# One program for attention and two mixture layers: the second layer's vector, scalar and GpSimd work issued by seven slots, and its weight sums cut in four

## The chip, the core and the metric

The kernel runs on one core of a Trainium2 chip. The core has TensorE (PE; its weight loads are listed apart as PEld), VectorE (DVE), ScalarE (ACT), GpSimd (POOL) and the queue of SyncE (SP), which issues nearly all DMAs here. The engines run on their own and meet at semaphores; each takes its instructions strictly in the order in which the program gives them. The metric is the device time of one execution in microseconds (us). The kernel before was run three times: 1477.61, 1478.47 and 1479.58 us, median 1478.47.

## What is computed

```python
attn = attention in chunks of 64 tokens       # batch 4, 8 heads, 576 tokens, head size 64
x = attn.reshape(2304, 512)
h = np.maximum(x @ w_in, 0.0)                 # first layer: 512 -> 2048
x = h * h @ w_out                             #              2048 -> 512
p = domain_probs / domain_probs.sum(-1)       # second layer: 4 experts
for e in range(4):
    h = np.maximum(x @ w1[e], 0.0)            # 512 -> 1024
    out += p[:, e:e + 1] * (h @ w2[e])        # 1024 -> 512
```

All matrices are float32. The kernel splits every operand of the large products into a rounded high part and the remainder (a low part), and adds three products (high by high, high by low, low by high), so each product stands as three matmuls.

## The kernel before

**First layer.** Attention, the first layer and the preparation of the second layer's weights are written as one row of ticks, `r` = 0 to 85. From tick 20 on a tick holds 12 matmuls of step `m` of the first product (`l1`) and 12 of step `m - 1` of the second (`l2`); 80 steps in all, over blocks of 384 or 512 tokens (8 of 20 steps have 384). Between them stands a chain: ACT takes the ReLU of PSUM into the tile `r` (L308), DVE squares it (L309), ACT rounds the high part (L313), DVE takes the low part (L314), and `l2` of the next tick reads both. The raw weights of the first layer arrive as float64 words; 20 blocks of them are turned into float32 after 170 us (L129 to L152), with three instructions of POOL for each block.

**Jobs.** The second layer's weights are four experts by four quarters of the 1024 columns, with two matrices each: 32 `job`s, one started every second tick from tick 20. Before the second layer can use Strassen's form (seven products of half matrices instead of eight), a job loads the four quarters (three DMAs), POOL forms four sums (L469), and the seven pieces are split into high and low parts and stored to DRAM. Before, a job moves on once at the end of every tick: load; one tick later the sums; one tick later the first half of the split (ACT rounds 896 columns at L475, DVE and POOL take the remainder of 448 columns each at L478, SP stores 896 KB at L481); one tick later the second half. All engines take their parts in program order, so an ACT instruction of a job stands between the ACT instructions of the chain above.

**Second layer.** 48 units `n`: three groups of 768 tokens, times four experts, times four quarters of the 1024 columns (`j` = 0 to 3). A unit has seven slots `u`. In a slot PE does six matmuls of 384 columns (`c_unit`, L525: one Strassen product of this unit's hidden values) and then nine of 256 columns (`d_unit`, L618: three products of the unit before; in slot 0 those of the unit two before). `c_finish` turns the seven sums in three PSUM banks (`b`, `c`, `d`) into seven pairs of high and low tiles: `s1` and `s3` are made by DVE in slot 5, `s2` by POOL from `s1`, and `s4` by DVE from `s2` in slot 6; `split` rounds on ACT (L558) and takes the remainder on POOL (L559). `d_finish` adds the finished banks of token block `t` into `uw` and the outputs: after product 6 the bank x = 1 into `uw` (DVE L655, in units with `j` = 0 ACT L653), after product 5 the bank x = 0 (DVE L657), then the scaled parts. When `j` = 3, `uw` is put into the outputs (L637, L683). PE may not go on in a bank's other half until the add that reads the whole bank is done. In slot 0 the products (2, 4) and (2, 2) need the adds that followed (2, 6) and (2, 5) in slot 6.

**What sets the order.** Nothing is scheduled by a program: each engine gets its instructions in the order in which this code runs. In a slot of before it is: PE's six, `c_finish` of this slot, then for each of three products its nine matmuls' share and its `d_finish`.

Of the kernel before, what the change touches and what calls it, by code (L numbers as in the profile page):

```python
# [18 lines left out]
P = 128  # L19
# [13 lines left out]
HALF = 384  # L33
# [11 lines left out]
def tile_kernel(ctx, tc, q, k, v, moe_w_in, moe_w_out, moe2_p, moe2_w1, moe2_w2, out):  # L45
# [245 lines left out]
    def l1(i):  # L291
# [4 lines left out]
        for kk in range(KD):  # L296
# [16 lines left out]
        nc.scalar.copy(hi[:, :T], r[:, :T])  # L313
        nc.vector.tensor_tensor(  # L314
            out=lo[:, :T], in0=r[:, :T], in1=hi[:, :T].bitcast(F32), op=ALU.subtract
# [100 lines left out]
    def y_split(sp, i):  # L416
        h, l = y_slot(i)
        a = comb[sp][i]
        nc.scalar.copy(h, a)
        eng = nc.vector if sp == 0 or i % 2 == 0 else nc.gpsimd  # L420
        eng.tensor_tensor(out=l, in0=a, in1=h.bitcast(F32), op=ALU.subtract)
        yield
# [17 lines left out]
    def job_load(which, n):  # L440
        e, j = divmod(n, NP)
        r = late["jb"].tile([P, 8, 2 * P], F32, tag="raw", name="jraw", bufs=2)
# [17 lines left out]
        1: ((4, 0, 3, ALU.add), (5, 4, 1, ALU.subtract), (6, 1, 0, ALU.subtract), (7, 2, 5, ALU.subtract)),  # L460
        2: ((4, 0, 1, ALU.subtract), (5, 3, 4, ALU.subtract), (6, 0, 3, ALU.subtract), (7, 2, 5, ALU.subtract)),
    }

    def job(which, n):

        r = job_load(which, n)
        yield
        for o, a, b, op in SUMS[which]:
            nc.gpsimd.tensor_tensor(out=r[:, o], in0=r[:, a], in1=r[:, b], op=op)  # L469
        yield  # L470
        c = NW // 2
        for part in range(2):
            x = r.rearrange("p s c -> p (s c)")[:, 2 * P + part * c:2 * P + (part + 1) * c]
            w = late["jb"].tile([P, 2, c], F32R, tag="split", name="jsplit", bufs=2)
            nc.scalar.copy(w[:, 0], x)  # L475
            for i, eng in enumerate((nc.gpsimd, nc.vector)):
                cs = slice(i * c // 2, (i + 1) * c // 2)
                eng.tensor_tensor(  # L478
                    out=w[:, 1, cs], in0=x[:, cs], in1=w[:, 0, cs].bitcast(F32), op=ALU.subtract
                )  # L480
            nc.sync.dma_start(out=kept[which, n][:, :, part * c:(part + 1) * c], in_=w.bitcast(F32))  # L481
            yield
# [20 lines left out]
    UNITS = ((0, Y11), (1, Y21), (4, T2), (3, T1), (5, T3), (6, Y22), (2, T4))  # L503
    A11, A12, A22, S1, S2, S3, S4 = range(7)
    B11, B21, B22, R1, R2, R3, R4 = range(7)
    g, st = {}, {}

    def c_unit(n, u):
        ws, ys = UNITS[u]
        if u == 0:  # L510
            st["b"] = bank("t")
# [4 lines left out]
        elif u == 1:  # L516
            st["c"] = bank("h")
        elif u == 3:
            st["d"] = bank("t")
        p = st["bcbdbdb"[u]][:, :HALF]  # L520
# [14 lines left out]
    def snap(nm, p):  # L535
        s = st[nm] = temp(nm)
        nc.scalar.copy(s, p)  # L537

    def keep(nm, p):
        s = st[nm] = temp(nm)  # L540
        nc.scalar.activation(out=s, in_=p, func=AF.Relu)

    def high(n, i, p):
        nc.scalar.activation(out=g[n][i][0], in_=p, func=AF.Relu)  # L544

# [6 lines left out]
    def relu_with(nm, p, other, op):  # L552
        s = st[nm] = temp(nm)
        nc.vector.scalar_tensor_tensor(out=s, in0=p, scalar=0.0, in1=st[other], op0=ALU.max, op1=op)  # L554

    def split(n, i, nm):
        h, l = g[n][i]
        nc.scalar.copy(h, st[nm])  # L558
        nc.gpsimd.tensor_tensor(out=l, in0=st[nm], in1=h.bitcast(F32), op=ALU.subtract)  # L559

    def c_finish(n, u):
        b, c, d = (st[x][:, :HALF] if x in st else None for x in "bcd")
        if u == 0:
            snap("u1", b)
        elif u == 1:
            nc.vector.tensor_tensor(out=c, in0=c, in1=st["u1"], op=ALU.add)
            high(n, A11, c)
            keep("a11", c)
            low(n, A11, c)
        elif u == 2:  # L570
            snap("u2", b)
        elif u == 3:
            snap("u3", d)
        elif u == 4:
            c = st["c"] = bank("h")
            c = c[:, :HALF]
            nc.vector.tensor_tensor(out=c, in0=b, in1=st["u3"], op=ALU.add)
            keep("a22", c)
            high(n, A22, c)
            low(n, A22, c)  # L580
        elif u == 5:
            nc.vector.tensor_tensor(out=d, in0=d, in1=st["u2"], op=ALU.add)
            relu_with("s1", d, "a22", ALU.add)
            relu_with("s3", d, "a11", ALU.subtract)
            s = st["s2"] = temp("s2")
            nc.gpsimd.tensor_tensor(out=s, in0=st["s1"], in1=st["a11"], op=ALU.subtract)  # L586
            split(n, S3, "s3")
            split(n, S2, "s2")
            split(n, S1, "s1")
        elif u == 6:  # L590
            high(n, A12, b)
            relu_with("s4", b, "s2", ALU.subtract)
            split(n, S4, "s4")

    def c_last(n):
        low(n, A12, st["b"][:, :HALF])
# [26 lines left out]
    owed = []  # L623

    def d_flush(n, t):
        sp, m = divmod(n, NU)
        e = m // NP
        r1 = rows[sp][t + 3]
        p1 = prob[:, r1 // P, e:e + 1]
# [283 lines left out]
```

## Time and profile before

| what | value |
|---|---|
| median of three runs | 1478.47 us |
| the profiled execution | 1476.51 us, of which the span is 1474.7 us |
| PE busy in the span | 1272.3 us (86%) |
| DVE, POOL, ACT busy | 897.2, 781.1, 652.4 us |
| first layer from tick 20 to its end | about 170 to 576.5 us |
| start of the second layer | 576.5 to 595.5 us |
| its units up to the last slot of products | 595.5 to 1451 us |
| mean granted TensorE clock | 0.949 |

A row of a timeline gives the start and the time of some instructions that follow one another, their engine, line, operation and tiles, and in square brackets how long the engine stood idle before them and what released it. A list of waits adds these idle times up. No engine but PE is busy for more than 61% of the span, and PE's idle time is what can be won. A PE that waits also loses time afterwards where the granted clock has fallen.

### The profile page before, as it was taken

The numbers are of one execution on the slowest core, as the hardware profiler recorded it, in microseconds if no ns is written. First come the engines' busy times: TensorE is split into PE (matmuls) and PEld (weight loads), VectorE is DVE, ScalarE is ACT, GpSimd is POOL, SyncE is SP. The second block draws the span as 40 slices with busy tenths as digits, with TensorE's granted clock in tenths as the row PEclk, the third lists the DMA queues.
The fourth block names the chain that finished last, engine by engine and source line by source line (L and its number), as shares of the span: only waits on it lengthen the run. The fifth ranks groups of instructions, "written<-read, shape, count | busy, mean of one in ns | idle before, by whom it ended". The sixth has DMA issues, their size and how long they took to land.

```text
span 1474.7 us, 22299 instructions
## 1 busy us (share of the span) xinstructions
PE 1272.3 (86%) x8344; PEld 1160.9 (79%) x8344; DVE 897.2 (61%) x1439; ACT 652.4 (44%) x1271; POOL 781.1 (53%) x771
## 2 busy tenths in 40 slices
PE   6999977987896998898988878988888889888896
PEld 5888866766675876888888878888888788888786
DVE  7866765586566556355656555656565556565655
ACT  5555543343343334444444444444444444444442
POOL 3400686676667466254655453556554535454544
PEclk8999989999999899899999999999999999999998
DMA  9752256676574666755556556556565465565642
GB/s 216 164 113 68 71 180 218 205 230 205 203 255 149 223 240 212 302 200 200 204 196 216 193 191 243 200 200 215 190 229 186 180 243 205 196 227 185 235 153 93
DMA packets 134972, 288.79 MB, mean 196 GB/s; under 512 B 64977, under 2 KB 93649, under 8 KB 128721
## 3 DMA queue, kind: packets, MB, share of 16 engines
q1 hardware_dynamic: 132240, 286.72, 57.5%
q8 instruction: 65, 1.06, 0.3%
q10 hardware_dynamic: 2624, 0.66, 0.2%
q14 instruction: 43, 0.34, 0.1%
HBM read 223.91 MB, written 63.44 MB: 195 GB/s over the span
## 4 chain that ended last, share of the span: by engine, by line
PE 40%; DVE 17%; POOL 13%; DMA 10%; issue 8%; ACT 8%; SPq 3%; POOLq 0%; DVEq 0%; ACTq 0%
PE psa L618 17%; PE pst L525 10%; DMA jraw<-in_moe_w 6%; POOL jraw L469 4%; PE psh L525 4%; DVE s L554 3%; PE psa L330 3%; POOL jsplit L478 3%; PE psh L298 3%; POOL s L586 3%; ACT ar L558 2%; ACT ar L544 2%; DMA w2d<-jsplit 2%; DVE uw L657 2%; DVE o L679 2%
## 5 line engine op out<-in xcount | busy, mean ns | idle before, releaser
L525 PE MATMUL pst<-ar 128*128 128x384 f32 x1728 | 350.2, 338 | 6.0 <-ACT u L537 3.4
L525 PEld LDWEIGHTS pst<-ar 128*128 128x128 f32 x1728 | 292.0, 190 | 6.7 <-ACT u L537 3.7
L330 PE MATMUL psa<-ar 128*128 128x512 f32 (+1 forms) x960 | 247.4, 397 | 56.0 <-ACT ar L313 32.7
L618 PE MATMUL psa<-w2x,ar 128*128 128x256 f32 x1512 | 216.2, 288 | 65.0 <-DVE uw L655 61.5
L618 PE MATMUL psa<-ar 128*128 128x256 f32 x1512 | 225.2, 293 | 54.3 <-DVE uw L655 28.7
L618 PEld LDWEIGHTS psa<-ar 128*128 128x128 f32 x1512 | 211.3, 198 | 66.7 <-DVE uw L655 32.4
L618 PEld LDWEIGHTS psa<-w2x,ar 128*128 128x128 f32 x1512 | 202.7, 195 | 76.9 <-DVE uw L655 69.1
L330 PEld LDWEIGHTS psa<-ar 128*128 128x128 f32 x960 | 180.2, 199 | 105.2 <-ACT ar L313 44.3
L667 POOL TENSOR_TENSOR o<-o,x 128x256 f32<-128x256 f32 x135 | 101.0, 748 | 240.0 <-ACT x L666 223.6
L559 POOL TENSOR_TENSOR ar<-s,ar 128x384 fp32r<-128x384 f32 x192 | 195.3, 1045 | 4.6 <-ACT ar L558 4.6
L558 ACT CAST ar<-s 128x384 fp32r<-128x384 f32 x192 | 93.7, 512 | 179.8 <-DVE s L554 170.8
L469 POOL TENSOR_TENSOR jraw<-jraw 128x256 f32<-128x256 f32 x128 | 108.8, 871 | 97.8 <-DMA jraw<-in_moe_w 95.3
L478 DVE TENSOR_TENSOR jsplit<-jraw,jsplit 128x448 fp32r<-128x448 f32 x64 | 63.9, 998 | 117.8 <-ACT jsplit L475 112.9
L657 DVE TENSOR_TENSOR uw<-psa,uw 128x512 f32<-128x512 f32 x144 | 95.1, 688 | 64.4 <-PE psa L618 47.6
L298 PE MATMUL pst<-ar 128*128 128x512 f32 (+1 forms) x576 | 132.1, 380 | 0.0
L298 PEld LDWEIGHTS pst<-ar 128*128 128x128 f32 x576 | 111.1, 197 | 14.6
L475 ACT CAST jsplit<-jraw 128x896 fp32r<-128x896 f32 x64 | 60.2, 940 | 115.0 <-POOL jraw L469 110.6
L143 POOL TENSOR_TENSOR raw<-raw 128x512 f32<-128x512 f32 x32 | 35.0, 1093 | 142.6 <-DVE raw L142 84.3
L548 DVE SCALAR_TENSOR_TENSOR ar<-psh,ar 128x384 fp32r<-128x384 f32 x96 | 53.6, 558 | 90.3 <-ACT ar L544 45.1
L537 ACT COPY u<-pst 128x384 f32<-128x384 f32 x144 | 69.1, 480 | 83.6 <-PE pst L525 81.2
L586 POOL TENSOR_TENSOR s<-s,a 128x384 f32<-128x384 f32 x48 | 48.9, 1019 | 107.4 <-DVE s L554 83.3
L314 DVE TENSOR_TENSOR ar<-r,ar 128x512 fp32r<-128x512 f32 (+1 forms) x80 | 76.2, 953 | 39.8 <-ACT ar L313 38.2
(112 smaller groups left out, 1878.1 us busy)
## 6 DMA issues: line engine op xcount, KB each, us to landing
ar<-w1d SPq DMA_DIRECT2D x48, 1792.0 KB, 7.3
ar<-w2d SPq DMA_DIRECT2D x48, 896.0 KB, 7.1
w2x<-w2d SPq DMA_DIRECT2D x48, 896.0 KB, 6.8
w1d<-jsplit SPq DMA_DIRECT2D x32, 896.0 KB, 4.9
w2d<-jsplit SPq DMA_DIRECT2D x32, 896.0 KB, 5.2
raw<-in_moe_w_in SPq DMA_DIRECT2D x16, 512.0 KB, 5.9
raw<-in_moe_w_out SPq DMA_DIRECT2D x16, 512.0 KB, 4.8
jraw<-in_moe_w SPq DMA_DIRECT2D x32, 256.0 KB, 5.2
```

The costliest lines, as they stand in the source:

```text
L298: nc.tensor.matmul(ph[:, :T], lhsT=w[:, kk, :], rhs=x[tb][:, kk, :], start=(kk == 0 and n == 0), stop=(kk == KD - 1 and n == 2),)
L314: nc.vector.tensor_tensor(out=lo[:, :T], in0=r[:, :T], in1=hi[:, :T].bitcast(F32), op=ALU.subtract)
L330: nc.tensor.matmul(o, lhsT=w, rhs=y, start=(f == 0 and n == 0), stop=(f == G - 1 and n == 2))
L469: nc.gpsimd.tensor_tensor(out=r[:, o], in0=r[:, a], in1=r[:, b], op=op)
L478: eng.tensor_tensor(out=w[:, 1, cs], in0=x[:, cs], in1=w[:, 0, cs].bitcast(F32), op=ALU.subtract)
L525: nc.tensor.matmul(p, lhsT=w[:, kk, :], rhs=y[:, kk, :], start=(kk == 0 and z == 0 and u in (0, 1, 3)), stop=(kk == 1 and z == 2 and u in ...
L558: nc.scalar.copy(h, st[nm])
L559: nc.gpsimd.tensor_tensor(out=l, in0=st[nm], in1=h.bitcast(F32), op=ALU.subtract)
L586: nc.gpsimd.tensor_tensor(out=s, in0=st["s1"], in1=st["a11"], op=ALU.subtract)
L618: nc.tensor.matmul(p, lhsT=w, rhs=y, start=(k in (1, 7) and z == 0), stop=(k in (3, 4) and z == 2), skip_group_check=True,)
L657: nc.vector.tensor_tensor(out=uw, in0=pb[n, t, 0], in1=uw, op=ALU.add)
L667: nc.gpsimd.tensor_tensor(out=o1[:, :2 * P], in0=o1[:, :2 * P], in1=x, op=ALU.add)
```

## The change

Four things change.

- **Slots.** `d_finish` is gone. Its parts have names (`B`: bank x = 1 into `uw`; `A`: bank x = 0; `x1`, `x0`: scaled copies; `o1`, `o0`, `O`: into the outputs; `W`, `F`: the end of an expert), and two tables, BEFORE and AFTER, say in which slot each is written, ahead of or behind the slot's nine matmuls. `c_finish` is cut into nine steps: slots 7 and 8 are slots 0 and 1 of the next unit. The `s4` pair and the low part of A12 move there. The splits of the next token group (`y_split`) are spread over slots 1 to 10.
- **Jobs.** A job now moves on by half ticks: the sums two ticks after the load, two quarters of the split at the end of the tick after the next, their stores half a tick later, the other two quarters half a tick after that. Each quarter is 448 columns on ACT, and its remainder is wholly POOL's or wholly DVE's. Three buffers each for the loaded and the split tiles, instead of two. One store is 448 KB; a job has four.
- **Squares.** From tick 20 on `l1` leaves the square in its PSUM bank instead of the tile `r`, and ACT and DVE read it there.
- The order of the seven weight pieces in memory is another one (UNITS, SUMS, R3 and B11 to R4). PE's instructions stand as before.

```diff
+        sq = r if "x" not in late else ph
         nc.vector.scalar_tensor_tensor(
-            out=r[:, :T], in0=ph[:, :T], scalar=0.0, in1=r[:, :T], op0=ALU.max, op1=ALU.mult
+            out=sq[:, :T], in0=ph[:, :T], scalar=0.0, in1=r[:, :T], op0=ALU.max, op1=ALU.mult
         )
...
-        yield
+        yield 4
         for o, a, b, op in SUMS[which]:
             nc.gpsimd.tensor_tensor(out=r[:, o], in0=r[:, a], in1=r[:, b], op=op)
-        yield
-        c = NW // 2
+        yield 3
+        c = NW // 4
...
-            w = late["jb"].tile([P, 2, c], F32R, tag="split", name="jsplit", bufs=2)
+            w = late["jb"].tile([P, 2, c], F32R, tag="split", name="jsplit", bufs=3)
             nc.scalar.copy(w[:, 0], x)
...
+            eng = nc.vector if part % 2 else nc.gpsimd
+            eng.tensor_tensor(out=w[:, 1], in0=x, in1=w[:, 0].bitcast(F32), op=ALU.subtract)
...
+            if part % 2:
+                yield 1
+                for o, w in done:
+                    nc.sync.dma_start(out=o, in_=w)
+                done = []
+                yield 1
...
+        elif at == 6:
             split(n, S3, "s3")
+            nc.scalar.activation(out=g[n][A12][0], in_=b, func=AF.Relu)
             split(n, S2, "s2")
+        elif at == 7:
             split(n, S1, "s1")
+            relu_with(n, "s4", b, "s2", ALU.subtract)
+            low(n, A12, b)
+        elif at == 8:
             split(n, S4, "s4")
...
+    BEFORE = {4: ((0, "o1"), (0, "W"), (1, "W")), 5: ((1, "o1"),), 7: ((2, "W"),), 8: ((2, "o1"),), 9: ((2, "o0"),)}
+    AFTER = {
+        1: ((0, "B"),), 2: ((1, "B"),), 3: ((0, "A"), (1, "A"), (0, "x1")), 4: ((0, "O"), (1, "x1")),
+        5: ((1, "O"),), 6: ((2, "B"), (2, "A")), 7: ((2, "x1"), (2, "x0"), (0, "F")), 8: ((1, "F"),),
+        10: ((2, "F"),),
+    }
+    SPLITS = {1: Y11, 2: Y21, 3: T2, 4: T1, 7: T3, 8: Y22, 10: T4}
```

On DVE in the second layer, at the end of an ordinary unit (slots 5 and 6, and the first of slot 0), there stood before, `s4` ahead of the two adds into `uw`:

```order
L554 SCALAR_TENSOR_TENSOR s1_6200<-pst_6145,a22_6176 128x384
L554 SCALAR_TENSOR_TENSOR s3_6202<-pst_6145,a11_6110 128x384
L679 SCALAR_TENSOR_TENSOR o_5142<-psa_6133,prob_149,o_5142 128x512
L554 SCALAR_TENSOR_TENSOR s4_6231<-pst_6075,s2_6204 128x384
L655 TENSOR_TENSOR uw_5143<-psa_6220,uw_5143 128x512
L657 TENSOR_TENSOR uw_5143<-psa_6235,uw_5143 128x512
L548 SCALAR_TENSOR_TENSOR ar_79<-pst_6075,ar_79 128x384
```

and now, at the same place:

```order
L547 SCALAR_TENSOR_TENSOR s1_5861<-pst_5806,a22_5838 128x384
L547 SCALAR_TENSOR_TENSOR s3_5863<-pst_5806,a11_5768 128x384
L657 SCALAR_TENSOR_TENSOR o_5334<-psa_5794,prob_149,o_5334 128x512
L629 TENSOR_TENSOR uw_5335<-psa_5873,uw_5335 128x512
L631 TENSOR_TENSOR uw_5335<-psa_5889,uw_5335 128x512
L547 SCALAR_TENSOR_TENSOR s4_5913<-pst_5729,s2_5865 128x384
L541 SCALAR_TENSOR_TENSOR ar_79<-pst_5729,ar_79 128x384
```

The two adds (`B`, `A`) have moved ahead of `s4`, which depends on POOL's `s2`; the order of the rest is the same here.

On DVE where an expert ends (`j` = 3), from the O of block 0 in slot 4, before:

```order
L679 SCALAR_TENSOR_TENSOR o<-psa,prob,o 128x512
L683 SCALAR_TENSOR_TENSOR o<-uw,prob,o 128x256
L632 SCALAR_TENSOR_TENSOR o<-uw,prob,o 128x256
L582 TENSOR_TENSOR pst<-pst,u_5773 128x384
L554 SCALAR_TENSOR_TENSOR s_5847<-pst,a_5820 128x384
L554 SCALAR_TENSOR_TENSOR s_5849<-pst,a_5752 128x384
L679 SCALAR_TENSOR_TENSOR o<-psa,prob,o 128x512
L683 SCALAR_TENSOR_TENSOR o<-uw,prob,o 128x256
L632 SCALAR_TENSOR_TENSOR o<-uw,prob,o 128x256
L554 SCALAR_TENSOR_TENSOR s_5880<-pst,s_5851 128x384
L655 TENSOR_TENSOR uw<-psa,uw 128x512
L657 TENSOR_TENSOR uw<-psa,uw 128x512
```

and now, from the O of block 1 in slot 5:

```order
L657 SCALAR_TENSOR_TENSOR o<-psa,prob,o 128x512
L629 TENSOR_TENSOR uw<-psa,uw 128x512
L631 TENSOR_TENSOR uw<-psa,uw 128x512
L547 SCALAR_TENSOR_TENSOR s_6089<-pst,s_6040 128x384
L541 SCALAR_TENSOR_TENSOR ar<-pst,ar 128x384
L660 SCALAR_TENSOR_TENSOR o<-uw,prob,o 128x256
L666 SCALAR_TENSOR_TENSOR o<-uw,prob,o 128x256
L568 TENSOR_TENSOR psh<-psh,u_6085 128x384
L660 SCALAR_TENSOR_TENSOR o<-uw,prob,o 128x256
L666 SCALAR_TENSOR_TENSOR o<-uw,prob,o 128x256
```

The writes of `uw` into the outputs (`F`, two instructions for each block) stood among `s1`, `s3` and `s4`, ahead of the two adds; they now come behind them, in the first slots of the next expert.

On ACT near the end of the first layer, before:

```order
L308 ACTIVATE r<-pst 128x512
L313 CAST ar<-r 128x512
L475 CAST jsplit<-jraw 128x896
L308 ACTIVATE r<-pst 128x512
L313 CAST ar<-r 128x512
```

and now:

```order
L309 ACTIVATE r<-pst 128x512
L314 CAST ar<-pst 128x512
L477 CAST jsplit<-jraw 128x448 x2
L309 ACTIVATE r<-pst 128x512
L314 CAST ar<-pst 128x512
```

One cast of 896 columns has become two of 448 at the same place, and the high part is rounded from the PSUM bank.

## Rows read from the trace of the kernel before

**Rows 1.** Busy time by stretch: first layer from tick 20, second layer's units.

```profile
core 0: us, PE busy (x) PEld busy (x) DVE busy (x) ACT busy (x) POOL busy (x), PEclk, DMA share, GB/s
170.00:576.50 406.50, 350.75 (x1514) 288.02 (x1513) 255.12 (x333) 163.56 (x261) 276.75 (x252) 0.95 0.61 203
...
595.50:1451.00 855.50, 741.87 (x4926) 718.34 (x4926) 498.45 (x829) 382.79 (x816) 441.78 (x460) 0.95 0.57 206
```

**Rows 2.** Waits of PE's weight loads, 620 to 1475: total us, times, longest.

```profile
PEld psa L618 <- DVE uw L655: 101.5, 36, 7.0
...
PEld psa L618 <- ACT uw L653: 23.3, 11, 2.1
```

**Rows 3.** Timeline of two ordinary units: slots, and the wait in slot 0.

```profile
915.28 1.21 PE L525 MATMUL pst<-ar 128*128 128x384 f32 x6
...
917.34 1.21 PE L525 MATMUL pst<-ar 128*128 128x384 f32 x6
...
932.05 1.21 PE L525 MATMUL pst<-ar 128*128 128x384 f32 x6
...
934.16 1.21 PE L525 MATMUL pst<-ar 128*128 128x384 f32 x6
...
944.00 0.56 DVE L554 SCALAR_TENSOR_TENSOR s<-pst,s 128x384 f32<-128x384 f32 x1 [1.43 <-ACT ar L544]
944.47 0.68 DVE L655 TENSOR_TENSOR uw<-psa,uw 128x512 f32<-128x512 f32 x1
...
945.21 0.61 PE L618 MATMUL psa<-ar 128*128 128x256 f32 x3 [1.38 <-DVE uw L655]
```

**Rows 4.** Timeline of PE: its waits in slot 0 over one expert, 982 to 1055.

```profile
982.54 1.70 PE L618 MATMUL psa<-ar 128*128 128x256 f32 x9 [1.80 <-ACT uw L653]
...
1035.10 2.45 PE L618 MATMUL psa<-w2x,ar 128*128 128x256 f32 x9 [3.79 <-DVE uw L655]
...
1054.55 1.70 PE L618 MATMUL psa<-ar 128*128 128x256 f32 x9 [1.80 <-ACT uw L653]
```

**Rows 5.** Waits in the first layer, 170 to 576.5: total us, times, longest.

```profile
ACT jsplit L475 <- POOL jraw L469: 108.0, 31, 7.6
...
POOL jraw L469 <- DMA jraw<-in_moe_w: 92.4, 23, 5.6
PEld psa L330 <- ACT ar L313: 44.0, 25, 5.5
...
PEld psa L330 <- DVE ar L314: 28.5, 37, 1.5
```

**Rows 6.** Timeline of ACT and PE near 346: one of the long waits.

```profile
343.16 0.94 ACT L475 CAST jsplit<-jraw 128x896 fp32r<-128x896 f32 x1 [5.19 <-POOL jraw L469]
...
346.16 0.69 PE L330 MATMUL psa<-ar 128*128 128x384 f32 x1 [4.39 <-ACT ar L313]
```

**Rows 7.** Timeline of PE's weight loads in dense ticks: 384 tokens, then 512.

```profile
487.25 2.09 PEld L298 LDWEIGHTS pst<-ar 128*128 128x128 f32 x12
489.33 2.09 PEld L330 LDWEIGHTS psa<-ar 128*128 128x128 f32 x12
...
526.60 2.68 PEld L298 LDWEIGHTS pst<-ar 128*128 128x128 f32 x12
529.32 2.68 PEld L330 LDWEIGHTS psa<-ar 128*128 128x128 f32 x12
```

**Rows 8.** Busy time in a stretch with four weight conversions, columns as Rows 1.

```profile
445.00:465.00 20.00, 14.48 (x62) 11.14 (x61) 17.75 (x20) 9.29 (x16) 18.08 (x16) 0.97 0.34 118
```

**Rows 9.** Groups by line, 170 to 576.5: busy us, mean ns.

```profile
L478 POOL TENSOR_TENSOR jsplit<-jraw,jsplit 128x448 fp32r<-128x448 f32 x62 | 83.8, 1352 | 9.9 <-ACT jsplit L475 9.9
...
L314 DVE TENSOR_TENSOR ar<-r,ar 128x512 fp32r<-128x512 f32 (+1 forms) x63 | 61.1, 971 | 33.1 <-ACT ar L313 31.6 <-PE psa L330 0.7
```

**Rows 10.** DMA issues: count, KB each, median us to landing.

```profile
w1d<-jsplit SPq DMA_DIRECT2D x32, 896.0 KB, 4.9
...
out<-o SPq DMA_DIRECT2D x18, 256.0 KB, 2.1
```

**Rows 11.** Landing of the stores at L481, 300 to 580.

```profile
DMA to landing us min/median/max: 4.0/5.1/10.1
```

**Rows 12.** Timeline at the start of the second layer.

```profile
585.34 0.48 ACT L537 COPY u<-pst 128x384 f32<-128x384 f32 x1 [2.33 <-POOL jsplit L478]
...
595.55 1.32 PE L525 MATMUL pst<-ar 128*128 128x384 f32 x6 [2.62 <-DMA ar<-w1d]
```

More of the change, by code (lines that the diff above doesn't have):

```diff
@@ L561, in c_finish @@
[L561 to L586, printed above, removed]
+        nc.scalar.copy(h, st[n, nm])
@@ new lines, in split, with c_finish @@
+        nc.gpsimd.tensor_tensor(out=l, in0=st[n, nm], in1=h.bitcast(F32), op=ALU.subtract)
+    def c_finish(n, at):
+        b, c, d = (st[n, x][:, :HALF] if (n, x) in st else None for x in "bcd")
+        if at in (0, 2, 3):
+            s = st[n, f"u{at}"] = temp(f"u{at}")
+            nc.scalar.copy(s, d if at == 3 else b)
+            if at == 2:
+                low(n, A11, c)
+        elif at in (1, 4):
+            if at == 4:
+                c = st[n, "c"] = bank("h")
+                c = c[:, :HALF]
+                nc.vector.tensor_tensor(out=c, in0=b, in1=st[n, "u3"], op=ALU.add)
+            else:
+                nc.vector.tensor_tensor(out=c, in0=c, in1=st[n, "u0"], op=ALU.add)
+            i, nm = (A11, "a11") if at == 1 else (A22, "a22")
+            nc.scalar.activation(out=g[n][i][0], in_=c, func=AF.Relu)
+            s = st[n, nm] = temp(nm)
+            nc.scalar.activation(out=s, in_=c, func=AF.Relu)
+        elif at == 5:
+            nc.vector.tensor_tensor(out=d, in0=d, in1=st[n, "u2"], op=ALU.add)
+            relu_with(n, "s1", d, "a22", ALU.add)
+            relu_with(n, "s3", d, "a11", ALU.subtract)
+            s = st[n, "s2"] = temp("s2")
+            nc.gpsimd.tensor_tensor(out=s, in0=st[n, "s1"], in1=st[n, "a11"], op=ALU.subtract)
+        elif at == 6:
@@ L621, in d_unit, with d_move @@
             )
[L623 to L629, printed above, removed]
-        o1, uw = late["o"][:, t + 3, :], late["uw"][:, t, :]
-        if e == 0:
-            nc.vector.scalar_tensor_tensor(
-                out=o1[:, :2 * P], in0=uw[:, :2 * P], scalar=p1, in1=o1[:, :2 * P], op0=ALU.mult, op1=ALU.add
-            )
-            nc.scalar.activation(out=o1[:, 2 * P:], in_=uw[:, 2 * P:], func=AF.Copy, scale=p1)
-        else:
-            nc.vector.scalar_tensor_tensor(out=o1, in0=uw, scalar=p1, in1=o1, op0=ALU.mult, op1=ALU.add)
-        if m == NU - 1:
-            nc.sync.dma_start(out=out[r1:r1 + P, :], in_=o1)
-    def d_finish(n, t, k):
+    def d_move(n, t, what):
         sp, m = divmod(n, NU)
@@ L780, in tile_kernel, with advance @@
         going = []
+        def advance(half):
+            for y in going[::-1]:
+                if y[0] == half:
+                    k = next(y[1], None)
+                    if k is None:
+                        going.remove(y)
+                    else:
+                        y[0] += k
         y0_at = LEAD + (npass1 - 1) * G * NB + 2 * G + LAG
@@ L793, in tile_kernel @@
             run_all(do(r, "load"))
+            if r >= JOB_AT and r % JOB_EVERY == 0 and work:
+                going.append([2 * r, job(*work.pop(0))])
+            advance(2 * r)
             if r < NTILE + LAG_A:
@@ L833, in tile_kernel @@
                 run(ch)
-            if r >= JOB_AT:
-                if work and (r - JOB_AT) % JOB_EVERY == 0:
-                    going.append(job(*work.pop(0)))
-                for y in going:
-                    next(y, None)
-        for y in going:
-            run(y)
+            advance(2 * r + 1)
+        for half in range(2 * r + 2, 2 * r + 12):
+            advance(half)
+        assert not going
         for _ in late.pop("y0"):
@@ L847, in tile_kernel @@
             sp, m = divmod(n, NU)
[L848 to L853 removed]
+            if m == 2 and n < NQ:
+                pend["y"] = y_gather() if sp == 1 else iter(())
             if m == 6 and sp + 1 < NSUP:
```

152 lines of the change are left out of this document (71 added, 81 removed).

## The prediction, made before the changed kernel had run

> **What bounds the kernel now.** I read the busy times by stretch first, then who waits for whom, then the timeline where the waits lie. Two stretches hold nearly everything that the change touches: the first layer from tick 20 on (406.5 us) and the second layer's units up to their last products (855.5 us) [rows 1]. In neither is DVE, ACT or POOL full over the whole stretch (POOL comes nearest, 276.75 of 406.5 us), so what counts is PE: what its matmuls need when nothing stands before them, and what is spent beyond.
>
> Second layer. A slot of PE takes 917.34 - 915.28 = 2.06 us in one unit and 934.16 - 932.05 = 2.11 us in the next [rows 3], 2.085 on average. From 595.5 to 1451 lie 47 units of seven slots: 329 x 2.085 = 686 us. The stretch takes 855.5, so 169.5 us are waits and the slow clock behind them. The list of waits says which: PE's weight loads stand 101.5 us on DVE's add of bank x = 1 (L655) and 23.3 us on the same add by ACT (L653) [rows 2]. An ordinary wait is shown in [rows 3]: DVE makes `s4` at 944.00 after 1.43 us of standing, only then the add at 944.47, and PE, idle for 1.38 us, goes on at 945.21. The add needed nothing of `s4`; it stood behind it. At an expert's end the wait is 3.79 us and the nine products then take 2.45 us where 1.70 and less stand elsewhere [rows 4]. Over one whole expert 1054.55 - 982.54 = 72.0 us pass [rows 4] for 28 slots of 58.4 us: 13.6 us lost, 163 over twelve experts, the rest of the 169.5 at the two changes of token group (longest wait 7.0 us [rows 2]).
>
> First layer. A dense tick takes 2 x 2.08 = 4.16 us with 384 tokens and 2 x 2.72 = 5.44 with 512 [rows 7]. The 1514 matmuls of the stretch [rows 1] are 63 ticks of 24, of which 24 have 384 tokens: 24 x 4.16 + 39 x 5.44 = 312 us. It takes 406.5; 94.5 us are lost. PE waits for ACT's high part (44.0 us) and DVE's low part (28.5) [rows 5]. Behind them stands a job: ACT sits 108.0 us in front of the job's cast until POOL has its sums, and POOL 92.4 us until the job's loads land [rows 5]. At 343.16 ACT began that cast after 5.19 us of standing; the ReLU, square and high part queued behind it, and PE lost 4.39 us at 346.16 [rows 6].
>
> **The change part by part.**
>
> *Second layer.* The work of each engine stays what it is: per unit, of 14.6 us, DVE has 498.45 / 47 = 10.6 us, ACT 8.1, POOL 9.4 [rows 1]. What moves is when. I laid the new order out by hand on slots of 2.085 us, with 0.68 for an add, 0.56 for the other DVE instructions. Product (2, 6) ends about 2.0 us into slot 6. DVE is then through with O of block 1, so the two adds run from 2.0 to 3.45, which is 1.4 us into the next slot 0; (2, 4) starts there at 1.05 and needs only the first (0.6), (2, 2) starts at 1.4 and needs the second. An ordinary unit so loses about 0.1 us instead of 2.24 (16.85 - 14.6). `s4` comes later, but its products stand in slot 4 and its pair is ready in slot 2. Moving the remainders of S1 and S4 on POOL by a slot costs nothing: (0, 5) and (0, 3) read them in slots 3 and 4, one slot later than they are ready.
>
> Where an expert ends, DVE gets six more instructions (`F`; at the 0.56 to 0.97 us of one in [rows 3, 9], 3.4 to 5.8 us), now behind the adds, in slots 0, 1 and 3, while the adds of x = 1 are ACT's. The last two reach into slot 4 and push the sum in bank c, then s1, s2, and ACT's add behind the cast of s2: by hand PE waits 1.8 us in slot 0 instead of the two waits of that expert beyond an ordinary unit. Once per expert: 1.8 + 3 x 0.1 = 2.1 us, twelve times 25. At each of the two changes of token group the splits add to three slots a DVE instruction of 768 columns (twice the 0.56 us of 384) and DVE's wait for ACT's copy: I put 5 us each, 10. So 35 of the 169.5 us stay; and waits of 1.4 us left the clock at 2.4 GHz in ordinary units, so its part goes too. Gain **133 us**. Bounds: 155 if only the 0.1 us per unit and little else stays; 105 if the expert's end and the group's change cost twice as much (70 - 6). No wait of the changed order is in the trace, so these come from durations.
>
> *Jobs.* Two more ticks (about 10 us) between loads and sums take POOL's 92.4 us of standing away, whose longest piece is 5.6 us [rows 5]; one and a half ticks between sums and casts (7 us) cover POOL's four sums. ACT's 108.0 us go with it. What is late next? First POOL itself: 276.75 us of work [rows 1] against 312 us, 89%, and where conversions of weights fall four in a row it is at 18.08 of 20 us already [rows 8]. Three such stretches exist; I leave 20 us of waits to them. Second, a new wait: with three split buffers and two quarters a tick, the second cast of a tick needs the buffer that a store of the tick before has left. The round is cast 0.5 (half of 0.94 [rows 6]), remainder on POOL 1.35 [rows 9], landing of the store, about 0.1 between; two rounds go into three ticks. With the 4.9 us of an 896 KB store [rows 10] a round is 6.85 and a tick 4.57: above 4.16, below 5.44 [rows 7], so 24 short ticks lose 0.4 us, 10 us. With the 2.1 us of a 256 KB store [rows 10] nothing is lost. With 10.1, the longest landing [rows 11], a tick becomes 8.0 and the layer 506 us. I take the 4.9, nearer in kind. The 64 more issues are SP's, beside PE's work.
>
> On that landing the Trainium skill speaks against the change: "DMA: Bandwidth & Descriptors" gives a transfer a fixed cost of about 2.0 us, so halves don't land in half the time. By it a store of 448 KB would land in about 2.0 + (4.9 - 2.0) / 2 = 3.45 us (an estimate from that page and the measured 4.9); the round would be 5.4, a tick 3.6, no wait would be left, and the sum would come out 10 us lower.
>
> *Squares.* DVE's low part reads PSUM instead of SBUF. Its mean is 971 ns [rows 9], while DVE's add of 512 columns with one operand in PSUM takes 680 [rows 3]: 0.3 us shorter in a chain for which PE waits 28.5 us [rows 5]. It is part of the gain here, not on top: PE waits for it after it has waited for the high part. The Trainium skill ("SBUF — State Buffer", on the shared port pair) says that a DVE instruction with two SBUF inputs and a GpSimd one lock each other out; by it the low part would no longer feel POOL at all.
>
> So the first layer keeps 20 + 10 and a few us of add-to-PSUM waits, 34.5 of the 94.5. Gain **60 us**; bounds 80 (half of POOL's 20, no store wait) and 25 (the store round at some 6.5 us of landing: tick 5.7).
>
> *Start and end.* At 585.34 the first ACT copy waited for the last job's split, and at 595.55 PE waited for the weights that SP loads behind the job's stores [rows 12]. The last job now ends about a tick later, partly overlapped: 3 us lost, between 0 and 5. At the end the two adds no longer stand behind F of blocks 0 and 1: 1 us gained.
>
> *Sum.* 1474.7 - 60 + 3 - 133 - 1 = 1283.7 us of span. The profiled execution took 1476.5 for a span of 1474.7, and the median lies 2.0 above it: 1283.7 + 1.8 + 2.0 = 1287.5, say **1287**.
>
> **The rivals.**
>
> *A. The adds still come late.* If DVE, with 0.2 us to spare in slots 5 to 0, slips by a slot's fraction that repeats, the ordinary unit keeps its 2.24 us: 47 x 2.24 = 105 of 169.5 stay, with the 10 at the changes of group. Gain 54 instead of 133: **1367**. For it: the tight second add. Against: DVE is busy 10.6 of 14.6 us, so a slip is caught up by slot 1.
>
> *B. The first layer gains nothing*, because POOL's backlog and the store round take the place of the wait for the sums: 1287 + 60 = **1347**. For it: POOL at 89%. Against: POOL's 92.4 us of standing for loads certainly goes.
>
> *C. Slower.* The store round becomes the bound of every tick. Before, a tick takes 406.5 / 63 = 6.45 us. A tick of (1.95 + L) x 2 / 3 must cost more than the 131 us won elsewhere: above 6.45 + 131 / 63 = 8.53 us, so L above 10.85 us. At L = 12 it is 9.3 us, 63 x 9.3 = 586 us, and the kernel takes 1478 + 179 - 131 = **1526**. Against: the longest landing of a store twice as large was 10.1, the median 5.1 [rows 11]; but half of them wait behind job loads.
>
> *D. Nothing changes*, about **1478**, were the order the same; the order shows that it isn't, and the two gains would have to be eaten exactly.
>
> **How the numbers follow.** Forecast 0.67, A 0.12, B 0.15, C 0.03, D 0.03. The forecast's own bounds: 1474.7 - 80 - 155 + 3.8, about 1243, to 1474.7 - 25 - 105 + 5 + 3.8, about 1354. That and B hold a little under 0.8, so the range goes on to A's 1367 and a little: **1243 to 1370**. Within 0.2% (3 us, about what a measurement of this kernel can tell from no change) lies D alone; slower is C: faster 0.94, same 0.03, slower 0.03.
>
> **What would show it.** Right: the waits of PE's weight loads on the adds of x = 1 fall from 125 to under 40 us, slots follow each other at 2.06 and 2.11 through slot 0, and the granted clock of the second layer rises from 0.95 to 0.98 or more; ACT no longer stands for POOL's sums, POOL no longer for job loads, and the stretch from tick 20 shrinks to some 346 us with POOL above 75%. A shows as PE waiting in every slot 0; B as a stretch of 400 us with ACT waiting for stores or POOL; C as casts that wait for stores for hundreds of us. I would be wrong most easily in the first layer's 34.5 us, which rest on POOL's bursts, and in the 35 us of the second.

## The result and the profile after

The changed kernel takes 1296.0 us (median; 1293.8 to 1298.9) where the kernel before took 1478.0 beside it: a ratio of 0.877 (95% interval 0.875 to 0.879). The forecast was 1287, the range 1243 to 1370. The sum was nearly right; its two large terms were not, in opposite directions, so that it lies so close is in part luck.

The profiled execution has a span of 1292.0 us. Its busy time by stretch, columns as in [rows 1]; the stretches are those of the stages after (first layer from tick 20, start of the second, its units, end):

```profile
170.00:545.00 375.00, 337.92 (x1513) 287.29 (x1512) 224.28 (x334) 169.36 (x323) 261.78 (x255) 0.95 0.67 221
545.00:563.00 18.00, 13.64 (x62) 12.12 (x60) 9.45 (x16) 7.49 (x15) 5.30 (x5) 0.91 0.79 291
563.00:1273.50 710.50, 698.20 (x4926) 690.22 (x4926) 500.12 (x830) 368.00 (x819) 452.51 (x464) 1.00 0.66 248
1273.50:1292.00 18.50, 9.73 (x72) 8.74 (x72) 12.29 (x18) 3.72 (x8) 11.45 (x13) 0.84 0.23 85
```

Beside [rows 1] the units of the second layer hold the same 4926 matmuls in 710.5 us instead of 855.5, at a granted clock of 1.00 instead of 0.95, with DVE, ACT and POOL as busy as before. The first layer's stretch is shorter by much less, and its clock is still 0.95. The waits of PE's weight loads in the second layer (total us, times, longest), which answer to [rows 2]:

```profile
PEld psa L610 <- ACT uw L627: 12.6, 12, 3.1
PEld psa L610 <- DVE uw L631: 4.3, 14, 0.4
PEld psa L610 <- DVE uw L629: 1.3, 2, 0.6
```

L629 is now DVE's add of the bank x = 1 (before L655), L627 the same by ACT (L653), and L631 the add of the bank x = 0, for which PE's weight loads stood before (620 to 1475, as [rows 2]):

```profile
PEld psa L618 <- DVE uw L657: 14.2, 39, 0.7
```

Of 101.5, 23.3 and 14.2 us are left 1.3, 12.6 and 4.3. The timeline of PE and DVE through an ordinary unit's end and slot 0, beside [rows 3]:

```profile
956.81 0.69 DVE L629 TENSOR_TENSOR uw<-psa,uw 128x512 f32<-128x512 f32 x1 [0.32 <-PE psa L610]
956.95 1.21 PE L529 MATMUL pst<-ar 128*128 128x384 f32 x6
957.60 0.69 DVE L631 TENSOR_TENSOR uw<-psa,uw 128x512 f32<-128x512 f32 x1
958.00 1.32 PE L610 MATMUL psa<-w2x,ar 128*128 128x256 f32 x9
958.21 0.55 DVE L547 SCALAR_TENSOR_TENSOR s<-pst,s 128x384 f32<-128x384 f32 x1
959.15 1.21 PE L529 MATMUL psh<-ar 128*128 128x384 f32 x6
```

The adds (L629, L631) come straight after the product, `s4` behind them; the slot takes 959.15 - 956.95 = 2.20 us, 0.1 more than an ordinary one, and no wait stands at PE.

In the first layer (170 to 545) the waits that answer to [rows 5] are:

```profile
DVE jsplit L479 <- ACT jsplit L477: 97.5, 42, 5.5
ACT jsplit L477 <- DMA w1d<-jsplit: 45.9, 19, 4.8
ACT jsplit L477 <- DMA w2d<-jsplit: 40.1, 21, 4.7
PEld psa L331 <- ACT ar L314: 39.7, 17, 4.9
PEld psa L331 <- DVE ar L315: 8.2, 20, 0.5
ACT jsplit L477 <- POOL jraw L470: 7.7, 3, 4.3
```

ACT's 108.0 us in front of POOL's sums have become 7.7. In their place ACT stands 86.0 us for the landing of the stores, and DVE 97.5 us for ACT's casts. PE still waits 39.7 us for the high part, where it was 44.0; only the wait for the low part has gone from 28.5 to 8.2.

Where the time went, stage by stage:

| stage | before | after | gain | forecast |
|---|---|---|---|---|
| up to the first product of the second layer | 576.5 | 546.3 | 30 | 60 |
| start, to the first units | 19.1 | 16.9 | 2 | -3 |
| units of the second layer | 855.5 | 710.5 | 145 | 133 |
| end | 23.7 | 18.5 | 5 | 1 |
| span | 1474.7 | 1292.0 | 182.7 | 191 |

### The profile page after: what moved, and what is told of

It is laid out like the page before. It is cut to its first block, busy times and chain, and to the rows that moved or that the text cites. A ratio compares the mean times of both kernels' runs of the same rounds, so it can differ in the third digit from the quotient of the medians.

```text
span 1292.0 us, 22549 instructions
## 1 busy us (share of the span) xinstructions
PE 1217.7 (94%) x8344; PEld 1133.6 (88%) x8344; DVE 866.3 (67%) x1437; ACT 641.6 (50%) x1335; POOL 773.5 (60%) x773
## 4 chain that ended last, share of the span: by engine, by line
PE 73%; DMA 8%; DVE 6%; ACT 4%; POOL 4%; issue 3%; SPq 2%; DVEq 0%; ACTq 0%; POOLq 0%
PE psa L610 25%; PE pst L529 21%; PE psa L331 10%; PE pst L298 5%; PE psh L298 4%; PE psh L529 4%; DMA w2d<-jsplit 3%; DMA w1d<-jsplit 2%; POOL jsplit L479 2%; DMA q<-in_q 1%; PE pst L274 1%; POOL raw L143 1%; DMA k<-in_k 1%; ACT jsplit L477 1%; PE pst L218 1%
## 5 line engine op out<-in xcount | busy, mean ns | idle before, releaser
L331 PE MATMUL psa<-ar 128*128 128x512 f32 (+1 forms) x960 | 238.1, 392 | 37.1 <-ACT ar L314 34.1
L331 PEld LDWEIGHTS psa<-ar 128*128 128x128 f32 x960 | 182.5, 198 | 73.9 <-ACT ar L314 39.7
L610 PE MATMUL psa<-ar 128*128 128x256 f32 x1512 | 212.7, 284 | 12.4 <-ACT uw L627 8.9
L610 PEld LDWEIGHTS psa<-ar 128*128 128x128 f32 x1512 | 201.0, 188 | 19.5 <-ACT uw L627 12.6
L610 PE MATMUL psa<-w2x,ar 128*128 128x256 f32 x1512 | 202.0, 278 | 0.6 <-DVE uw L629 0.4
L610 PEld LDWEIGHTS psa<-w2x,ar 128*128 128x128 f32 x1512 | 195.7, 188 | 2.3 <-DVE uw L629 0.6
L631 DVE TENSOR_TENSOR uw<-psa,uw 128x512 f32<-128x512 f32 x144 | 95.1, 687 | 66.7 <-ACT uw L627 31.7
L479 DVE TENSOR_TENSOR jsplit<-jraw,jsplit 128x448 fp32r<-128x448 f32 x64 | 56.4, 881 | 110.1 <-ACT jsplit L477 102.1
L477 ACT CAST jsplit<-jraw 128x448 fp32r<-128x448 f32 x128 | 71.0, 567 | 106.7 <-DMA w1d<-jsplit 46.3
L629 DVE TENSOR_TENSOR uw<-psa,uw 128x512 f32<-128x512 f32 x108 | 74.6, 691 | 55.6 <-PE psa L610 55.2
L479 POOL TENSOR_TENSOR jsplit<-jraw,jsplit 128x448 fp32r<-128x448 f32 x64 | 77.5, 1211 | 56.0 <-ACT jsplit L477 48.4
L570 ACT ACTIVATE ar<-psh 128x384 fp32r<-128x384 f32 x96 | 47.3, 492 | 124.4 <-DVE psh L566 66.2
```

The source lines that it names most:

```text
L331: nc.tensor.matmul(o, lhsT=w, rhs=y, start=(f == 0 and n == 0), stop=(f == G - 1 and n == 2))
L479: eng.tensor_tensor(out=w[:, 1], in0=x, in1=w[:, 0].bitcast(F32), op=ALU.subtract)
L610: nc.tensor.matmul(p, lhsT=w, rhs=y, start=(k in (1, 7) and z == 0), stop=(k in (3, 4) and z == 2), skip_group_check=True,)
L629: nc.vector.tensor_tensor(out=uw, in0=b, in1=uw, op=ALU.add)
L631: nc.vector.tensor_tensor(out=uw, in0=pb[n, t, 0], in1=uw, op=ALU.add)
```

## Experiments on the second layer

**The adds behind `s4`.** The kernel before, with `s4` and its split behind the adds of slot 6, nothing else:

```diff
-            relu_with("s4", b, "s2", ALU.subtract)
-            split(n, S4, "s4")
...
+        relu_with("s4", st["b"][:, :HALF], "s2", ALU.subtract)
+        split(n, S4, "s4")
```

> The kernel before with one thing moved: s4 and its split are written behind the adds of slot 6 (where the low part of A12 stands). Theory (the adds waited because they stood behind s4): the 36 units that don't end an expert lose their 1.5 to 1.8 us wait and the small one behind it, 36 x 2.24 = 80 us, so about 1398 us; the waits at an expert's end stay. Rival (work has to be a whole slot away everywhere, and one move only shifts the wait to the next instruction): less than 30 us won, above 1448 us.

It took 1406.7 us, ratio 0.952 (0.950 to 0.954): 72 us for two lines moved, where 80 were expected.

**The sums into the outputs as well.** The same, with every sum of `uw` into the outputs at an expert's end (F, L637 and L683) three slots later, behind the adds:

```diff
+                owed.append([3, d_flush, (n, t)])
...
+                for y in owed:
+                    y[0] -= 1
+                ready = [y[1:] for y in owed if y[0] == 0]
```

> The kernel before, with the fourth weight sum's split behind the adds (as in e_b_s4) and, besides, the unit's sum of uw into the outputs three slots later, behind the adds too. Theory: each of the second layer's waits is an add queued behind a wait of its own engine; with the second such place gone too most of the rest goes: 1406.7 less 50 to 60, about 1345 to 1355 us; the 10 to 15 us left of the second layer are those at the changes of the token group, where the splits of y still stand in one row. Rival: the sum into the outputs isn't in the way; the time stays within 10 us of 1406.7.

It took 1364.8 us, ratio 0.924 (0.922 to 0.925): 42 us more, 10 short of what was expected. From one unit's second slot to the next one's, read from the timelines of PE (us; the usual values, without the first expert, with which the layer begins):

| units | before | `s4` moved | F too | after |
|---|---|---|---|---|
| ordinary, two parities | 16.7, 16.9 | 14.7, 14.9 | 14.7, 14.9 | 14.6, 14.9 |
| second of an expert | 18.4 to 18.8 | 16.2 to 17.9 | 16.8 to 18.7 | 15.4 to 16.8, behind a change 18.4 |
| first of an expert | 18.5 to 19.7 | 18.0 to 19.2 | 14.7 | 14.6 |
| at a change of token group, two units | 22.9, 20.7 | 22.1, 19.9 | 22.1, 15.9 | 15.0, 14.7 |

So the rows of the table have causes of their own: `s4` held the ordinary unit by 2.0 us, F the first unit of an expert by some 4, and something else the change of group by some 8 us, at each of two changes. The second unit of an expert, too, is one to two microseconds shorter after than with both moves, some 17 us over the layer; no run tried what does that.

**The splits of the next token group in a row again.** The kernel after, with the seven splits behind the steps of slots 0 to 6 of one unit, as before:

```diff
                     c_finish(n, u)
+                    if m == NU - 1 and sp + 1 < NSUP:
+                        run(y_split(sp + 1, UNITS[u][1]))
```

> The kernel after, with the splits of the next token group in seven slots in a row behind the slot's own steps, as before. Theory: in e_b_s4_f the two units at each change of group took 22.1 and 15.9 us where after takes 14.96 and 14.69, so spreading the splits is worth about 8.4 us at each change: 1296 + 17 = 1313 us. Rival: in the new order the adds no longer stand behind them and the row costs little; within 5 us of 1296.

It took 1299.2 us, ratio 0.880 (0.878 to 0.881): 3 us slower, at the edge of what can be told. The rival held, and the 8 us are not the row's. The timeline of the kernel before at the first change of group shows what they are:

```profile
865.03 0.92 ACT L558 CAST ar<-s 128x384 fp32r<-128x384 f32 x2 [0.95 <-POOL s L586]
865.86 0.83 ACT L419 CAST ar<-acc 128x768 fp32r<-128x768 f32 x1
866.72 1.00 DVE L421 TENSOR_TENSOR ar<-acc,ar 128x768 fp32r<-128x768 f32 x1 [3.18 <-ACT ar L419]
...
871.20 0.68 DVE L655 TENSOR_TENSOR uw<-psa,uw 128x512 f32<-128x512 f32 x1
871.93 2.44 PE L618 MATMUL psa<-ar 128*128 128x256 f32 x9 [6.72 <-DVE uw L655]
```

ACT waits for POOL's `s2`; the cast of the next group's piece (L419 at 865.86) stands behind the cast of `s2`; DVE waits 3.18 us for it before it can take the remainder; and the add for which PE waits stands behind DVE's remainder. The change also moves the casts of `s3` and `s2` from slot 5 to slot 6, and gives the remainders of the T pieces to POOL. Both are in the diff, and the expectation read only the spreading. The run above has both: in it the same piece is in the same slot and its remainder still DVE's, but neither stands behind `s2` any more, and DVE does not wait:

```profile
786.69 0.84 ACT L420 CAST ar<-acc 128x768 fp32r<-128x768 f32 x1
787.82 0.95 DVE L422 TENSOR_TENSOR ar<-acc,ar 128x768 fp32r<-128x768 f32 x1
```

That these two are the whole of the 8 us is read from the timelines; no run tried either by itself.

## Experiments on the first layer

**Jobs as before.** The kernel after with the jobs' old steps, at their old place in the tick: one step a tick, halves of 896 columns, two buffers each. Of the edit:

```diff
-        yield 4
+        yield 2
...
-        yield 3
-        c = NW // 4
+        yield 2
+        c = NW // 2
...
-            eng = nc.vector if part % 2 else nc.gpsimd
-            eng.tensor_tensor(out=w[:, 1], in0=x, in1=w[:, 0].bitcast(F32), op=ALU.subtract)
+            for i, eng in enumerate((nc.gpsimd, nc.vector)):
```

> The changed kernel with the jobs as they were before: one step a tick, two casts of 896 columns, two buffers each. Second layer and squares in PSUM stay changed. Theory (the 30 us that the first layer gained come from the jobs' new steps): 1296 + 25 to 35, about 1326 us, ACT again waiting some 100 us for POOL's sums. Rival (they come from the squares in PSUM): 1296 to 1306 us.

It took 1328.8 us, ratio 0.900 (0.898 to 0.901), 33 us above after; ACT stands for POOL's sums again (waits from 170 to 560):

```profile
ACT jsplit L476 <- POOL jraw L470: 145.9, 30, 9.2
```

**Squares as before**, in the tile `r`:

```diff
-        sq = r if "x" not in late else ph
+        sq = r
```

> The kernel after, with one thing put back: the squares of the two remainder products in layer 1 go into the float32 tile r in SBUF again, in place of PSUM. Theory: the layer-1 gain of about 30 us comes from the order of the jobs' splits, so the squares alone are worth 5 to 10 us: 1301 to 1306 us, with the low part on DVE near 970 ns again where it is 640 ns now. Rival: the squares carry most of the gain; then the time rises by 20 us or more, to 1316 or above.

It took 1305.1 us, ratio 0.883 (0.881 to 0.884): 9 us. The low part's group of after, whose tile is in one of two PSUM banks, and of this run (busy us, mean ns):

```profile
L315 DVE TENSOR_TENSOR ar<-pst,ar 128x512 fp32r<-128x512 f32 (+1 forms) x48 | 30.8, 642 | 22.1 <-ACT ar L314 21.4
```

```profile
L315 DVE TENSOR_TENSOR ar<-r,ar 128x512 fp32r<-128x512 f32 (+1 forms) x62 | 59.5, 959 | 32.4 <-ACT ar L314 30.9 <-PE psa L331 0.7
```

The two parts, 33 and 9 us, are more than the 30 that the layer has gained, so they are not independent. With the old jobs and the squares in PSUM the second layer's first product starts at 581 us, no earlier than in the kernel before (576.5): beside the old jobs the squares win nothing that shows. The new steps carry the gain, and the squares' 9 us come with them. Which part of the new steps does it (the later sums, the smaller pieces, the third buffer) no run separates.

**A longer store round.** A fourth buffer for the splits needs room; two instead of three buffers of the first layer's own conversion make it, and their price is taken by a run of its own:

```diff
-CV_BUFS = 3
+CV_BUFS = 2
```

> The changed kernel with two instead of three buffers for the conversion of first-layer weights (CV_BUFS); it frees room that the next run needs, and is its control. Theory (ACT stands for the stores of the split quarters) and rival (POOL's backlog where weights are converted) both expect the changed kernel's time, 1296 us, within 4; if conversions need the third buffer, up to 10 us more.

It took 1300.6 us, ratio 0.880 (0.878 to 0.882). Then with the fourth buffer:

```diff
-CV_BUFS = 3
+CV_BUFS = 2
...
-            w = late["jb"].tile([P, 2, c], F32R, tag="split", name="jsplit", bufs=3)
+            w = late["jb"].tile([P, 2, c], F32R, tag="split", name="jsplit", bufs=4)
```

> As e_cv2, with four buffers for the split quarters instead of three, so that a cast needs the buffer whose store went out two ticks before. Theory (the store round of the prediction holds the first layer): ACT's 86 us of waits for stores fall below 15, PE's waits for ACT in the first layer from 39.7 us to under 20, and the time is 10 to 25 us below e_cv2. Rival (POOL's backlog in the stretches with conversions holds it, and the wait for the store only shows it): the waits move to another name and the time stays within 3 us of e_cv2.

It took 1276.0 us, ratio 0.864 (0.862 to 0.865): 24.6 us less than its control and 20 less than the changed kernel. Its waits, 165 to 545:

```profile
DVE jsplit L479 <- ACT jsplit L477: 44.8, 39, 3.1
PEld psa L331 <- ACT ar L314: 24.5, 17, 3.9
ACT jsplit L477 <- DMA w2d<-jsplit: 12.6, 17, 1.7
ACT jsplit L477 <- DMA w1d<-jsplit: 11.6, 16, 2.1
```

The store round was the larger part of the wait: ACT stands 24 us for landings, where it is 63 in the control and 86 in the changed kernel. The waits did not fall as far as expected (24 us for landings and not below 15, 24.5 us of PE's for the high part and not under 20), the time did.

**The remainders of a tick exchanged between DVE and POOL**, in the kernel after:

```diff
-            eng = nc.vector if part % 2 else nc.gpsimd
+            eng = nc.gpsimd if part % 2 else nc.vector
```

> The kernel after, with the engines of two quarters of a job's remainder exchanged: the first quarter's on DVE, the second quarter's on POOL, so that the store which the conversion a tick later waits for is no longer issued behind POOL. Theory (the store round is long because POOL's split is late): ACT's waits for the landing of the stores fall from 86 us in sum to about half, the time to about 1283 us. Rival: DVE's split comes as late as POOL's, or the round is the store's own landing; then the time is within 3 us of 1296.

It took 1283.1 us, ratio 0.868 (0.867 to 0.870). The time is the theory's, the mechanism is not: ACT still stands 80 us for landings.

```profile
POOL jsplit L479 <- ACT jsplit L477: 45.3, 25, 5.0
ACT jsplit L477 <- DMA w1d<-jsplit: 45.0, 19, 5.0
ACT jsplit L477 <- DMA w2d<-jsplit: 35.3, 21, 4.7
PEld psa L331 <- ACT ar L314: 30.7, 15, 4.7
DVE jsplit L479 <- ACT jsplit L477: 18.9, 15, 3.8
```

What fell is DVE's standing for a job's cast, 97.5 to 18.9 us. With DVE on the tick's first cast, its remainder is done while ACT waits, and the square of the next step no longer comes behind it: DVE now stands 51.8 us for the ReLU itself (L310 behind L309), where it was 8.4. On top of the longer buffers the same exchange,

```diff
-            eng = nc.vector if part % 2 else nc.gpsimd
+            eng = nc.gpsimd if part % 2 else nc.vector
```

> e_cv2_split4 with the engines of the two remainders of a tick exchanged, as in e_swap. Theory: DVE, which makes the chain's squares and low parts, stands 44.8 us in front of its remainder there because it belongs to the second of two casts; as the first cast's partner it doesn't, and part of the 13 us that this gave without the longer buffers comes again: 1264 to 1272 us. Rival: with four buffers the second cast is no longer late, and the exchange changes nothing (within 3 us of 1276).

changed nothing: 1274.9 us, ratio 0.863 (0.861 to 0.865). The rival held: with four buffers the second cast waits at most 1.0 us for a landing, and the exchange has little to win.

**What is left: POOL's sums or DVE?** Three variants of the version with four buffers. The third sum on DVE:

```diff
+            eng = nc.vector if i == 2 else nc.gpsimd
```

> e_cv2_split4 (four buffers for the splits, two for the conversions), with the third weight sum of a job in layer 1 on DVE in place of POOL. Theory: what is left of TensorE's waits in layer 1 there (24.5 us for the activations on ACT) stands behind POOL's bursts; with POOL's work a quarter less the time falls 5 to 15 us below 1276. Rival: DVE is as full as POOL; no change within 3 us, or slower.

1300.2 us, ratio 0.880 (0.878 to 0.882): 24 us slower, against the theory. The third sum overwrites a quarter that POOL's first sum reads, so DVE stood 54.4 us in front of it:

```profile
DVE jraw L471 <- POOL jraw L471: 54.4, 23, 5.3
```

The first sum, which needs only the loads:

```diff
+            eng = nc.vector if i == 0 else nc.gpsimd
```

> e_cv2_split4 with the first sum of a job on DVE instead of the third. The work moved is the same as in e_cv2_split4_sum, which took 1300 us and where DVE stood 54.4 us in front of that sum for POOL; the first sum needs the loads alone. Theory: what cost there was DVE's standing, not its work; without it the time is 1265 to 1277 us. Rival: DVE has no room for 31 sums of about 0.55 us in this layer; then it stays near 1300.

1281.5 us, ratio 0.868 (0.866 to 0.869). The same work without that standing costs 5 us instead of 24; in these 5 is also POOL's standing for the sum that DVE now makes (21.2 us). The forecast's upper end (1277) was passed by 4. And one sum left out, on no engine:

```diff
+            if i == 2:
+                continue
```

> e_cv2_split4 with the third sum of every job left out, so that the piece R4's neighbour at index 0 stays a raw quarter and the second layer's result isn't the reference's; POOL has a quarter less of sums and no other engine gets one. Theory: the waits for the high part on ACT that are left in layer 1 (24.5 us at the weight loads) stand behind POOL's bursts; the time falls from 1276 to 1262 to 1270 us. Rival: they stand behind the waits of ACT and DVE for each other, and POOL's load has little part in them; then the time is within 4 us of 1276.

1273.3 us, ratio 0.862 (0.860 to 0.863): 3 us less, hardly more than the spread of such runs, with POOL busy 246.86 us instead of 272.05 in the same 360 us (170 to 530). The rival held: a quarter of POOL's sums has little part in what is left. The longest wait of the version with four buffers shows what has; its timeline of ACT, DVE and PE:

```profile
335.41 0.48 ACT L309 ACTIVATE r<-pst 128x384 f32<-128x384 f32 x1
336.21 0.84 DVE L142 TENSOR_SCALAR raw<-cv 128x512 int32<-128x512 int32 x1
...
338.59 1.08 DVE L742 TENSOR_TENSOR prob<-dp,psum__148 128x72 f32<-128x72 f32 x1
...
339.60 1.55 DVE L479 TENSOR_TENSOR jsplit<-jraw,jsplit 128x448 fp32r<-128x448 f32 x1
341.07 0.55 DVE L310 SCALAR_TENSOR_TENSOR pst<-pst,r 128x384 f32<-128x384 f32 x1
...
342.23 1.00 PE L331 MATMUL psa<-ar 128*128 128x384 f32 x2 [3.66 <-ACT ar L314]
```

The ReLU is done at 335.9, its square begins at 341.07: between them DVE works off a weight conversion, the probabilities and a job's remainder without a gap. DVE's queue ahead of the square is thus the likely rest. No run took work from DVE alone, so this is read and not shown.

## Why the prediction was right, and where it was not

The total fits because errors cancel: the first layer gave 30 us less than forecast, the second 12, the start 5 and the end 4 more.

**Second layer: mechanism right, 12 us too little.** That the adds stood behind `s4` and F, and that the order frees them, was confirmed by the two runs on the kernel before (72 and 42 us). The ordinary unit's 0.1 us is the measured 0.1. Of the forecast's 35 us that stay, 24.5 do. The step that failed is the 10 us for the two changes of token group: the units there take 15.0 and 14.7 us, hardly more than others, so the pieces of 768 columns on DVE and its waits for ACT's copies, which the sum charged, cost next to nothing. What a change does cost comes a unit later and was not in the sum. ACT may not write the new group's outputs before those of the old are stored; its copy into `uw` stands behind that, and PE behind the copy:

```profile
819.27 0.48 ACT L639 ACTIVATE o<-psa,prob 128x256 f32<-128x256 f32 x1 [2.40 <-DMA out<-o]
...
822.61 1.70 PE L610 MATMUL psa<-ar 128*128 128x256 f32 x9 [2.42 <-ACT uw L627]
```

At the second change ACT stands 3.17 us and PE 2.75. The expert's end was put at 2.1 us, 1.8 of them for its own waits; its second unit costs 0.8 to 2.2 more than an ordinary one, and behind a change of group 3.6 to 3.8.

**First layer: half of the gain, by the mechanism of rival B in part.** POOL's waits for loads and ACT's for the sums went as said: of POOL's 92.4 us for loads none is left, though the sums come only one tick later than before and not two, as the prediction has it. The squares were worth their small share. The stretch from tick 20 shrank to 375 us and not to 346, with POOL busy for 70% of it and not above 75%.

What failed is the store round. It was built as cast 0.5, remainder 1.35, landing 4.9 and 0.1, in all 6.85 us, and two rounds were spread evenly over three ticks; that made a tick of 4.57 us and a loss of 10 us. The order does not spread them evenly. With three buffers, the second cast of a tick takes the buffer that the first cast of the tick before has filled, one tick earlier, while the first cast takes one that was filled nearly two ticks earlier. Of ACT's 86.0 us for landings, 85.5 stand before second casts (39 of the 40 waits, counted in the trace of the kernel after). The forecast's own numbers say as much once the spacing is right: a second cast has a tick and a cast's time, 4.7 or 6.0 us, for a round of 6.85; 24 short and 39 long ticks make some 84 us of waiting for ACT (an estimate from the prediction's rows; not all of ACT's waiting is PE's loss, and that it meets the 86 so well is partly chance, since the rounds vary). Some rounds are also much longer than the sum of their steps, because POOL takes up the remainder late. The timeline of the kernel after, one such round:

```profile
301.33 3.82 POOL L470 TENSOR_TENSOR jraw<-jraw 128x256 f32<-128x256 f32 x4
...
301.84 0.56 ACT L477 CAST jsplit<-jraw 128x448 fp32r<-128x448 f32 x1
...
304.43 0.57 ACT L477 CAST jsplit<-jraw 128x448 fp32r<-128x448 f32 x1 [2.02 <-DMA w2d<-jsplit]
...
305.12 1.43 POOL L143 TENSOR_TENSOR raw<-raw 128x512 f32<-128x512 f32 x1
...
308.51 0.56 ACT L477 CAST jsplit<-jraw 128x448 fp32r<-128x448 f32 x1
...
309.36 1.33 POOL L479 TENSOR_TENSOR jsplit<-jraw,jsplit 128x448 fp32r<-128x448 f32 x1
...
313.73 0.56 ACT L477 CAST jsplit<-jraw 128x448 fp32r<-128x448 f32 x1 [4.66 <-DMA w2d<-jsplit]
314.20 0.59 ACT L309 ACTIVATE r<-psh 128x512 f32<-128x512 f32 x1
...
317.21 4.08 PE L331 MATMUL psa<-ar 128*128 128x512 f32 x8 [4.47 <-ACT ar L314]
```

The casts at 301.84 and 308.51, the first of their ticks, find their buffers free; those at 304.43 and 313.73, the second, wait. The cast at 301.84 has its remainder on POOL only at 309.36, behind four sums and a conversion; the store follows, and the cast at 313.73 that needs the buffer comes 11.9 us after the first, not 6.85. The ReLU at 314.20 stands behind it, and PE loses 4.47 us. The prediction counted POOL's burst and the store round as two terms, 20 and 10 us; here they are one, and the burst lengthens the round. But this is one of the long rounds: on average POOL begins a remainder 2.0 us after its cast has ended, in half the cases within 0.9. And the exchange of DVE and POOL above, which takes the first cast's remainder from POOL, left 80 of the 86 us. So the spacing carries the wait, and POOL's queue adds to it. The fourth buffer, which gives every cast two ticks, brings 24.6 us back; the second layer's first product then starts at 528 us, 48 us earlier than in the kernel before, where the forecast was 60.

On the landing itself the rule of the Trainium skill ("DMA: Bandwidth & Descriptors", section "Anatomy of one DMA") fared well, though the section gives its fixed cost for DMAs that GpSimd issues, and SP issues the stores here. The stores of 448 KB at L484, 170 to 545:

```profile
DMA to landing us min/median/max: 2.9/3.8/9.1
```

The estimate worked out from that section's fixed cost was 3.45 us, the value taken 4.9, measured 3.8. But what it gave for the sum, no wait at all, fell with the same even spacing. The rule of the Trainium skill on the shared port pair ("SBUF — State Buffer", section "Terms") agrees with the low part's 640 ns against 959 with both inputs in SBUF, and the traces separate it from the operand's place as such. In the kernel before, both inputs in SBUF, the low parts of 512 columns took 692 to 696 ns where POOL did nothing meanwhile (11 of them, 170 to 545) and 967 to 1610 beside an instruction of POOL (23). After, one input in PSUM, they took 690 to 693 ns beside POOL (34), no more than without it.

**Start and end.** The last job did not come later by a tick's worth; 3 us lost were 2 gained. The end gave 5 instead of 1, since it held two waits like those of the units (2.43 us at 1454 and 3.08 at 1466 before, 0.43 each after). **Rivals.** A, late adds, did not show. B is half right: the store round, not POOL's sums, took the place of the wait. C asked for landings of 10.85 us; the median is 3.8, the longest 9.1.

## What to carry to other kernels

On an engine that takes its instructions in order, the price of an instruction is what it waits for, paid by all that stand behind it: put what another engine waits for ahead of whatever waits itself, and give the side work of the engines in the chain a slot in which its inputs are surely there. When buffers rotate through several engines and a store, add up the whole round with the queue in front of each step, not the steps alone, and hold it against the shortest time between two uses of a buffer, not the mean; one more buffer can be worth more than a faster step. The version with four buffers runs at 1276 us and beats both kernels.

## What was not expected

A store of half the size landed in 3.8 us where the whole took 4.9 [rows 10]: halving it saved 1.1 us. And the granted clock of the second layer went from 0.95 to 1.00, the full 2.4 GHz, with the longest of PE's waits on the adds at 3.1 us instead of 7.0. So part of the 145 us, some 44, is matmuls that run faster: PE's busy time for the same 4926 fell from 741.87 to 698.20 us.
